# Block-sparse attention feeding a squared-ReLU layer: rounding x, whole rows' scores, one copy of fixed keys and three products with v put at other places of the issue order

## The chip, the cores and the metric

The kernel runs on one core of a Trainium2 chip. The metric is the time of one execution on the device in microseconds (us), here the median of several runs. A run of the profiler gives the trace of one execution.

## The reference

```python
scores = scale * np.matmul(q, k.transpose(0, 1, 3, 2))     # B=4, H=8, S=768, D=64
mask = np.abs(blk_i - blk_j) <= 1                           # blocks of 32: the window
mask = mask | (blk_i == 0) | (blk_j == 0) | (blk_i == n_blocks - 1) | (blk_j == n_blocks - 1)
for qb in range(n_blocks):
    for kb in sampled_blocks[qb]:                           # 3 random blocks per query block
        mask[qb * 32:(qb + 1) * 32, kb * 32:(kb + 1) * 32] = True
attn = softmax(np.where(mask, scores, -1e9))
x = (attn @ v).transpose(0, 2, 1, 3).reshape(3072, 512)
h = np.maximum(x @ w_in, 0.0)                               # 512 x 2048
return (h * h @ w_out).astype(np.float32)                   # 2048 x 512
```

The first and the last query block of each batch see every key (whole rows). Every other query block sees at most eight blocks of keys: the first, the last, three sampled ones and three of the window.

## The kernel before, in words

The 3072 tokens are 24 tiles of 128 tokens, numbered k = 0 to 23, six for each batch; three tiles make a chunk c (384 tokens, eight chunks). The attention of a tile is done in two halves of four heads, called (k, u) with u 0 or 1 (class `Half`). The whole rows of a batch are done by four pairs of heads (class `Whole`).

**The dense layer** of a chunk is the generator `moe(c)`. `turn(c)` rounds x: for each of the three tiles ScalarE (ACT) writes a rounded copy xh (line 808), and VectorE (DVE) the remainder xl (line 809). Then come 16 column blocks f. `hidden(c, f)` makes 12 matmuls on TensorE (PE, line 820) into one PSUM bank ph, then Relu on ACT (r, line 824), the square on ACT (gh, line 831), the square again on DVE (gf, line 836), and the remainder gl on GpSimd (POOL, line 838). `project(c, f)` makes 9 matmuls (line 858) with gh, gl and the split output weights, and runs two blocks behind `hidden`: the last two blocks of a chunk are projected at the start of the next `moe`. Weights are split into two parts by ACT or DVE (788, 790) and POOL (791). Chunk 0 projects unsplit (line 848).

**The order of the work is written by hand.** Each engine runs its instructions in the order in which the program issues them. `moe` yields after every piece: 4 matmuls of `hidden` or one third of `project`; a block has 6 pieces and a chunk 96. After each yield the loop counts `now` up by one and lets a `Stream` issue whatever steps of the attention are due. A `Half` or `Whole` is a generator that yields the number of pieces to its next step (`LAG`).

A `Half` of a late tile (k of 6 and above, "moved") issues: scores (line 381) and loads; after one piece the maxima (393) and the subtraction p (401), which frees the two score banks; after 4 more pieces 16 exponentials on ACT, one per piece (426), a transpose on DVE into a tile pT (432), and 11 pieces later (`v`) the products with v on PE (pv, 476), the normalization on DVE (490 to 493, 325), and the loads of v for the next tile on the DMA queue of SyncE (SP; 301, 314). In the same piece the scores of a later half are due: halves start 16 pieces apart. Before the third group of exponentials `next_keys` may copy the fixed keys (first and last block) for a coming half into its tile KG (line 288). For tiles below 6 the copy stands right behind the exponentials.

A `Whole` starts `G_AT` = 9 pieces behind a half. It issues scores (g, 567), one piece later the maxima (581 to 585), 4 pieces later two exponentials pg (592), 4 pieces later eight pieces of copies by ACT and POOL (603), 5 pieces after the last of them a transpose on DVE into a tile pTg (609), and `w` = 16 pieces later its products with v (pvg, 637) and its normalization (648 to 656). The second pair of heads also loads the other half of v (`load_vn`, 222). pT and pTg share one tag with two buffers.

Scores, ph, pv and pvg take the five banks of one PSUM pool in turn: an allocation waits until the readers of the fifth allocation before it are done.

At a chunk's end the order is: the last four matmuls of `hidden(c, 15)`, r, gh, gf, gl, a yield (so the attention steps that are due), `turn(c+1)`, three pieces of `project(c, 14)`, three of `project(c, 15)`, the output, and `hidden(c+1, 0)`, which reads xh and xl. In pieces counted through, `turn(1)` stands at piece 90, `turn(3)` at 282, `turn(5)` at 474.

Of the kernel before, what the change touches and what calls it, by code (L numbers as in the profile page):

```python
# [32 lines left out]
NF = DFF // P  # L33
# [30 lines left out]
STEP = PIECES // (2 * UC)  # L64
EARLY = 23
LAST = 4
LAG = {"s": 0, "e": 4, "v": 11, "x": 4, "t": 4, "c": 0, "v0": 13, "w0": 4, "w": 16, "n": -1}

G_AT = 9

STEP_0 = 5
STEP_1, FIRST_1 = 12, 0
LAG_1 = {**LAG, "v": 10, "x": 3, "t": 6, "v0": 5, "n": 0}
LAG_0 = {"s": 2, "x": 2, "t": 3, "c": 2, "v0": 2, "n": 2}
# [22 lines left out]
def tile_block_sparse_attention_moe(ctx: ExitStack, tc, kd, knd, qd, qgd, vd, vnd, samp, const, wcat, out):  # L97
# [9 lines left out]
    nc = tc.nc  # L107
# [7 lines left out]
    def bank(name):  # L115
        return ps.tile([P, 512], F32, tag="s", name=name)
# [167 lines left out]
    def static_keys(b, t, u, copy=nc.scalar.copy):  # L284

        src = st["kn", b, u][:, 0 : NBLK : NBLK - 1].rearrange("p i a c -> p i (a c)").unsqueeze(1)
        dst = st["kg", b, t][:, :, 0:2, 2 * u : 2 * u + 2].rearrange("p j i a c -> p j i (a c)")
        copy(dst, src.broadcast_to(list(dst.shape)))
# [40 lines left out]
    class Half:  # L329
# [10 lines left out]
        def run(self, bank, lag):  # L340

            self.scores()
            self.loads(0)
            yield lag["s"]
            self.maxima()
            if self.moved:
                yield lag["e"]
                yield from self.turn_blocks()
                yield lag["v"]
            else:  # L350
                yield lag["x"]
                self.exps()
                self.next_keys()
                yield lag["t"]
                pt = self.turn(bank)
                yield lag["c"]
                self.copies(pt)
                self.loads(1)
                yield lag["v0"]
            po = self.values(bank)  # L360
            if lag["n"] >= 0:
                yield lag["n"]
            self.norm(po)
            self.loads(2)
# [43 lines left out]
        def next_keys(self):  # L408

            b, t = order[min(self.k + self.u, len(order) - 1)]  # L410
            if b > 0 and t < 2:
                static_keys(b, t, 1 - self.u)

        def turn_blocks(self):

# [32 lines left out]
        def turn(self, bank):  # L448
            pt = [bank(f"pt{self.name}_{e}") for e in range(2)]
            n = self.rows.stop  # L450
            for e in range(2):
                for i in range(2):
                    for c in range(2):
                        a = (2 * i + c) * P
                        nc.tensor.transpose(pt[e][:, a : a + n], self.p[:n, 2 * e + i, c], ident[:n, :n])  # L455
            return pt
# [208 lines left out]
    def units(c):  # L665
# [8 lines left out]
        both = [(at + i * STEP, u) for i, u in enumerate(halves)]  # L674
        both += [(at + i * STEP + G_AT, u) for i, u in enumerate(wholes)]
        return sorted(both, key=lambda x: x[0])
# [104 lines left out]
    def need(f, part):  # L781
        while done - AHEAD - 2 <= cuts.index((f, part)):
            cut_next()

    def split(c, src, name):
        w = rot.tile([P, 2, DM], F32R, tag="w", name=name, bufs=WBUFS)
        if c == 0:
            nc.scalar.copy(w[:, 0], src)  # L788
        else:
            nc.vector.tensor_copy(w[:, 0], src)  # L790
        nc.gpsimd.tensor_tensor(w[:, 1], src, w[:, 0], op=ALU.subtract)  # L791
        return w

    def split_wo(c, f):
        if c == 0:
            need(f, 1)
            if f < PLAIN:
                return
        wo[c, f] = split(c, WO[f], f"wo{c}_{f}")
# [12 lines left out]
    def hidden(c, f):  # L812
        xh, xl = xs[c]
        wi = (wi1.pop((c, f)) if f in SINGLE else WI[f]).rearrange("p a (c m) -> p a c m", c=NCC)
        ph = bank(f"ph{c}_{f}")
        steps = []
        for cc in range(NCC):
            steps += [(wi[:, 0, cc], xh[:, cc]), (wi[:, 0, cc], xl[:, cc]), (wi[:, 1, cc], xh[:, cc])]
        for i, (w, x) in enumerate(steps):
            nc.tensor.matmul(ph[:, :TOK], w, x, start=(i == 0), stop=(i == len(steps) - 1))  # L820
            if i % 4 == 3 and i < len(steps) - 1:
                yield 0.7
        r = pool["x"].tile([P, TOK], F32, tag="r", name=f"r{c}_{f}", bufs=2)
        nc.scalar.activation(r, ph[:, :TOK], AF.Relu)  # L824
        if c == 0 and f < PLAIN:
            gt[c, f] = pool["x"].tile([P, TOK], F32, tag="gh", name=f"gp{c}_{f}", bufs=3)
            nc.scalar.activation(gt[c, f], r, AF.Square)
            yield 0.7
            return
        gh = pool["x"].tile([P, TOK], F32R, tag="gh", name=f"gh{c}_{f}", bufs=3)  # L830
        nc.scalar.activation(gh, r, AF.Square)  # L831
        gf = pool["x"].tile([P, TOK], F32, tag="gf", name=f"gf{c}_{f}", bufs=2)
        if c == 0:
            nc.scalar.activation(gf, r, AF.Square)
        else:
            nc.vector.scalar_tensor_tensor(gf, ph[:, :TOK], 0.0, r, op0=ALU.max, op1=ALU.mult)  # L836
        gl = pool["x"].tile([P, TOK], F32R, tag="gl", name=f"gl{c}_{f}", bufs=3)
        nc.gpsimd.tensor_tensor(gl, gf, gh, op=ALU.subtract)  # L838
        gt[c, f] = (gh, gl)
        yield 0.7  # L840

    def project(c, f):
        if f == 0:
            acc[c] = [ps_o.tile([P, 512], F32, tag="o", name=f"po{c}_{u}") for u in range(UC)]
        if c == 0 and f < PLAIN:
            g = gt.pop((c, f))
            for u in range(UC):
                nc.tensor.matmul(  # L848
                    acc[c][u], g[:, u * P : (u + 1) * P], WO[f], start=(f == 0), stop=(f == NF - 1)
                )  # L850
                yield 0.85
            return
        gh, gl = gt.pop((c, f))
        w = wo.pop((c, f))
        for u in range(UC):
            at = slice(u * P, (u + 1) * P)
            for i, (g, k) in enumerate(((gh, 0), (gh, 1), (gl, 0))):
                nc.tensor.matmul(  # L858
                    acc[c][u], g[:, at], w[:, k], start=(f == 0 and i == 0), stop=(f == NF - 1 and i == 2)
                )  # L860
            yield 0.68

    def emit_out(c):
        po = acc.pop(c)
        o = [rot.tile([P, DM], F32, tag="x", name=f"ot{c}_{u}", bufs=5) for u in range(UC)]
        rows = [out[(c * UC + u) * P : (c * UC + u + 1) * P] for u in range(UC)]
        if c < NCH - 1:
            for u in range(UC):
                (nc.vector.tensor_copy if u == 1 else nc.scalar.copy)(o[u], po[u])
                nc.sync.dma_start(rows[u], o[u])  # L870
            return
        nc.vector.tensor_copy(o[0], po[0])
        nc.sync.dma_start(rows[0], o[0])
        nc.scalar.copy(o[1], po[1])
        nc.scalar.dma_start(rows[1], o[1])
        for i, copy in enumerate((nc.scalar.copy, nc.vector.tensor_copy)):
            at = slice(i * DM // 2, (i + 1) * DM // 2)
            copy(o[2][:, at], po[2][:, at])
            (nc.sync if i else nc.scalar).dma_start(rows[2][:, at], o[2][:, at])

    def moe(c):


        if c < NCH:
            turn(c)
        if c > 0:
            for f in range(NF - LEAD, NF):
                if c == 1 and f == NF - 1:
                    split_wo(0, f)
                yield from project(c - 1, f)  # L890
            emit_out(c - 1)
        if c == NCH:
            return
        for f in range(NF):
            for n in (f, f + 1) if f == 0 else (f + 1,):
                if n < NF:
                    if c == 0:
                        need(n, 0)
                    if n in SINGLE:
                        wi1[c, n] = split(c, W1[n], f"wi{c}_{n}")  # L900
            if c == 0 and f > 0:
                split_wo(c, f - 1)
            if f >= LEAD:
                yield from project(c, f - LEAD)
            if c > 0:
                split_wo(c, f)
            yield from hidden(c, f)
# [59 lines left out]
    for c in range(1, NCH):  # L967
        for at, u in units(c):
            work.add(at, c, lambda u=u, lag=LAG_1 if c == 1 else LAG: u.run(bank, lag))
    now = 0  # L970
# [71 lines left out]
```

## Time and profile before

| | us |
|---|---|
| median of 3 runs | 752.5 (749.96 to 754.48) |
| the profiled execution | 753.05 |
| its span in the trace | 751.3 |
| PE busy in the span | 714.9 (95%) |
| ACT, DVE, POOL busy | 519.0, 517.4, 498.8 |

The mean granted clock of PE is 0.991. A timeline row gives the start, the time, the engine, the line, the operation, output and inputs, the count, and in brackets the idle time of the engine ahead of it with what ended it. PEld is the loading of weights, which overlaps PE. A row of waits gives who waited for whom, the total, the number of waits and the longest. A row of a stage gives its bounds and length, busy time and count of PE, PEld, DVE, ACT and POOL, the granted clock, the DMA share and GB/s. SPq is the DMA queue of SyncE.

### The profile page before, as it was taken

How to read it: one execution, taken by the hardware profiler on the slowest of the kernel's cores; microseconds unless marked ns; L12 is line 12 of the kernel's file. 1: busy time of each engine (PE TensorE's matmuls, PEld its weight loads, DVE VectorE, ACT ScalarE, POOL GpSimd, SP SyncE). 2: the span in 40 equal slices, each digit the busy share in tenths (PEclk: the TensorE clock that was granted, in tenths of full speed). 3: DMA queues.
4: the chain of work that ended last, by engine and by line, in shares of the span. 5: the costliest groups of instructions: out<-in, count | busy, mean ns of one | idle time of the engine just before them, and what ended most of it. 6: DMA issues, size and time to landing. Idle time of an engine off the chain costs nothing.

```text
span 751.3 us, 24248 instructions
## 1 busy us (share of the span) xinstructions
PE 714.9 (95%) x8904; PEld 590.0 (79%) x8904; DVE 517.4 (69%) x1060; ACT 519.0 (69%) x1145; POOL 498.8 (66%) x624
## 2 busy tenths in 40 slices
PE   4678999999899999999999999999999999999997
PEld 2556776568788888877887888886888888888986
DVE  4895977758777676667878676577869676556452
ACT  4995786898676776578886777668986785623222
POOL 6952644238667576776866576766876675777885
PEclk9998999999999999999999999999999999999999
DMA  8775789653523445534343343645244343101001
GB/s 272 223 220 144 222 237 337 172 146 91 147 53 100 131 93 170 165 84 116 98 122 105 80 131 97 214 94 142 74 121 116 82 126 73 34 1 43 1 1 43
DMA packets 85755, 92.43 MB, mean 123 GB/s; under 512 B 13539, under 2 KB 73444, under 8 KB 85636
## 3 DMA queue, kind: packets, MB, share of 16 engines
q1 hardware_dynamic: 79684, 68.03, 34.6%
q0 software_dynamic: 5664, 22.45, 8.9%
q8 instruction: 71, 1.16, 0.7%
q14 instruction: 48, 0.39, 0.2%
q10 hardware_dynamic: 288, 0.39, 0.1%
HBM read 84.53 MB, written 6.29 MB: 121 GB/s over the span
## 4 chain that ended last, share of the span: by engine, by line
PE 82%; ACT 6%; DVE 5%; DMA 3%; issue 2%; SPq 1%; POOL 1%; ACTq 0%; POOLq 0%; DVEq 0%
PE ph L820 34%; PE po L858 28%; PE s L381 7%; PE pv L476 5%; PE po L848 4%; DMA V<-in_v_dram 2%; PE pvg L637 2%; ACT pm L426 1%; PE g L567 1%; DVE m L393 1%; PE pt L455 1%; SPq L314 1%; ACT V L209 1%; DMA kn<-in_kn_dram 1%; DVE p L401 1%
## 5 line engine op out<-in xcount | busy, mean ns | idle before, releaser
L820 PE MATMUL ph<-xh,wi 128*128 128x384 f32 x832 | 238.7, 348 | 0.0
L426 ACT ACTIVATE pm<-p 32x256 f32<-32x256 f32 x528 | 219.2, 415 | 17.8 <-DVE p L401 10.7
L858 PE MATMUL po<-wo,gh 128*128 128x512 f32 x672 | 212.0, 397 | 0.0
L791 POOL TENSOR_TENSOR wi<-W,wi 128x512 fp32r<-128x512 f32 x104 | 143.3, 1378 | 68.8 <-ACT wi L788 36.2
L824 ACT ACTIVATE r<-ph 128x384 f32<-128x384 f32 x128 | 62.9, 492 | 170.5 <-PE ph L820 169.6
L791 POOL TENSOR_TENSOR wo<-WO,wo 128x512 fp32r<-128x512 f32 x112 | 145.0, 1295 | 50.8 <-DVE wo L790 49.2
L838 POOL TENSOR_TENSOR gl<-gf,gh 128x384 fp32r<-128x384 f32 x112 | 117.7, 1051 | 87.1 <-DVE gf L836 74.5
L820 PEld LDWEIGHTS ph<-xh,wi 128*128 128x128 f32 x832 | 151.2, 188 | 13.1 <-issue 5.7
L836 DVE SCALAR_TENSOR_TENSOR gf<-ph,r 128x384 f32<-128x384 f32 x112 | 62.2, 555 | 140.9 <-ACT r L824 130.0
L858 PEld LDWEIGHTS po<-wo,gh 128*128 128x128 f32 x672 | 123.7, 189 | 24.4 <-issue 5.8
L820 PE MATMUL ph<-xl,wi 128*128 128x384 f32 x416 | 141.5, 340 | 0.0
L858 PE MATMUL po<-wo,gl 128*128 128x512 f32 x336 | 133.2, 396 | 0.8 <-POOL gl L838 0.8
L820 PEld LDWEIGHTS ph<-xl,wi 128*128 128x128 f32 x416 | 78.2, 188 | 10.0 <-issue 6.5
L790 DVE CAST wo<-WO 128x512 fp32r<-128x512 f32 x112 | 84.2, 752 | 0.0
L858 PEld LDWEIGHTS po<-wo,gl 128*128 128x128 f32 x336 | 63.3, 188 | 18.1 <-POOL gl L838 4.3
L393 DVE TENSOR_REDUCE m<-s 128x2 f32<-128x512 f32 (+1 forms) x96 | 61.1, 676 | 8.8 <-PE s L381 8.7
L831 ACT ACTIVATE gh<-r 128x384 fp32r<-128x384 f32 x112 | 58.9, 526 | 9.0
L476 PEld LDWEIGHTS pv<-V,pT 128*32 128x32 f32 x2816 | 43.8, 111 | 22.7 <-issue 12.9
L476 PE MATMUL pv<-V,pT 128*32 128x65 f32 x2816 | 53.1, 223 | 7.4 <-ACT pT L465 2.9
L820 PE MATMUL ph<-xh,WI 128*128 128x384 f32 x192 | 55.1, 348 | 2.1 <-ACT xh L808 2.1
L381 PE MATMUL s<-KG,q 64*32 64x160 f32 x1408 | 50.0, 304 | 5.4 <-issue 3.6
L401 DVE TENSOR_TENSOR p<-s,m 128x512 f32<-128x512 f32 (+1 forms) x72 | 45.9, 676 | 0.0
(89 smaller groups left out, 906.9 us busy)
## 6 DMA issues: line engine op xcount, KB each, us to landing
craw<-in_w_dram POOLq DMA_DIRECT2D x32, 512.0 KB, 5.9
V<-in_v_dram SPq DMA_DIRECT2D x462, 32.5 KB, 1.9
KG<-in_k_dram SPq DMA_DIRECT2D x198, 64.0 KB, 1.9
V<-in_v_dram SPq DMA_DIRECT2D x28, 390.0 KB, 4.3
q<-in_q_dram SPq DMA_DIRECT2D x24, 256.0 KB, 2.7
out_dram<-ot SPq DMA_DIRECT2D x22, 256.0 KB, 3.7
V<-in_v_dram SPq DMA_DIRECT2D x16, 292.5 KB, 4.6
vn<-in_vn_dram SPq DMA_DIRECT2D x5, 780.0 KB, 5.6
```

The lines of the kernel that those rows point to most:

```text
L381: nc.tensor.matmul(self.sb[e][g * BLK : (g + 1) * BLK, i * NSLOT + a : i * NSLOT + z], q[r, j, pr, :], k, start=True, stop=True,)
L393: nc.vector.tensor_reduce(m[at, e], self.sb[e][at].rearrange("p (i c) -> p i c", i=2), axis=AX, op=ALU.max)
L426: nc.scalar.activation(p[a * BLK : (a + 1) * BLK, g], x[g * BLK : (g + 1) * BLK, :, a], AF.Exp, scale=SCALE)
L476: nc.tensor.matmul(po[h * BLK : (h + 1) * BLK, g * VW : (g + 1) * VW], self.pT[:, g, 2 * e + i, c], v[:, self.u, j, h * VW : (h + 1) * VW] ...
L790: nc.vector.tensor_copy(w[:, 0], src)
L791: nc.gpsimd.tensor_tensor(w[:, 1], src, w[:, 0], op=ALU.subtract)
L820: nc.tensor.matmul(ph[:, :TOK], w, x, start=(i == 0), stop=(i == len(steps) - 1))
L824: nc.scalar.activation(r, ph[:, :TOK], AF.Relu)
L831: nc.scalar.activation(gh, r, AF.Square)
L836: nc.vector.scalar_tensor_tensor(gf, ph[:, :TOK], 0.0, r, op0=ALU.max, op1=ALU.mult)
L838: nc.gpsimd.tensor_tensor(gl, gf, gh, op=ALU.subtract)
L858: nc.tensor.matmul(acc[c][u], g[:, at], w[:, k], start=(f == 0 and i == 0), stop=(f == NF - 1 and i == 2))
```

## The change

Four edits of the issue order:

1. The yield behind the last block's squares goes, and one comes in behind `turn` of the next chunk: xh and xl now follow r, gh, gf and gl directly, and the attention steps of that piece come after them. The number of pieces is the same.
2. `G_AT` goes from 9 to 6 and `w` from 16 to 19: everything of a `Whole` moves up three pieces, but its products with v stay at their piece.
3. For tiles below 6 the copy of fixed keys goes from ACT to POOL. With the condition on the batch this is one copy: the one for half (6, 0), issued by half (5, 1).
4. For the halves (7, 0), (14, 0) and (15, 0) the products with v, the normalization and the loads behind them come two pieces earlier. For (7, 0) and (14, 0) that is the piece of the products of a `Whole`, right behind them.

```diff
-LAG = {"s": 0, "e": 4, "v": 11, "x": 4, "t": 4, "c": 0, "v0": 13, "w0": 4, "w": 16, "n": -1}
+LAG = {"s": 0, "e": 4, "v": 11, "x": 4, "t": 4, "c": 0, "v0": 13, "w0": 4, "w": 19, "n": -1}
-G_AT = 9
+G_AT = 6
+APART = 2
+SPLIT = ((7, 0), (14, 0), (15, 0))
...
                 yield from self.turn_blocks()
-                yield lag["v"]
+                yield lag["v"] - APART * ((self.k, self.u) in SPLIT)
...
             if b > 0 and t < 2:
-                static_keys(b, t, 1 - self.u)
+                static_keys(b, t, 1 - self.u, nc.scalar.copy if self.moved else nc.gpsimd.tensor_copy)
...
             nc.scalar.activation(gt[c, f], r, AF.Square)
-            yield 0.7
+            if f < NF - 1:
+                yield 0.7
             return
...
         gt[c, f] = (gh, gl)
-        yield 0.7
+        if f < NF - 1:
+            yield 0.7
...
         if c < NCH:
             turn(c)
         if c > 0:
+            yield 0.7
             for f in range(NF - LEAD, NF):
```

## The prediction

> **What bounds the kernel now.** I read the page first, then PE's waits from 60 us to the end, then the timeline around each wait.
>
> ```profile
> PE 714.9 (95%) x8904; PEld 590.0 (79%) x8904; DVE 517.4 (69%) x1060; ACT 519.0 (69%) x1145; POOL 498.8 (66%) x624
> q8 instruction: 71, 1.16, 0.7%
> ```
> ```profile
> PE s L381 <- issue: 3.6, 2, 2.0
> PE s L381 <- ACT pg L592: 2.9, 3, 1.4
> PE ph L820 <- ACT xh L808: 2.1, 1, 2.1
> PE s L381 <- ACT KG L288: 1.7, 2, 1.3
> PE ph L820 <- DVE xl L809: 1.1, 3, 0.4
> PE po L858 <- POOL gl L838: 0.8, 3, 0.3
> PEld pv L476 <- issue: 10.4, 35, 0.4
> ```
>
> PE is the bound: 95% busy, and behind the first 60 us it stands still only in the first six of these waits, 12.2 us (one of them, the 2.1 us for xh, is chunk 0's own start, which the change doesn't touch). Nothing else limits: so every wait that goes shortens the span by its length, and no matmul is removed. The rest of the working goes wait by wait.
>
> **Part 4, the three products moved up.** The 3.6 us "issue" are two gaps, each ahead of the last few score matmuls of a half.
>
> ```profile
> 194.68 0.92 PE L637 MATMUL pvg<-vn,pTg 128*64 128x65 f32 x24
> 197.12 1.11 PE L476 MATMUL pv<-V,pT 128*32 128x65 f32 x64
> 198.04 0.37 SPq L222 DMA_DIRECT2D vn<-in_vn_dram  x1
> 201.30 0.46 PE L381 MATMUL s<-KG,q 64*32 64x160 f32 x3 [1.96 <-issue]
> 399.91 0.92 PE L637 MATMUL pvg<-vn,pTg 128*64 128x65 f32 x24
> 402.35 1.11 PE L476 MATMUL pv<-V,pT 128*32 128x65 f32 x64
> 406.24 0.46 PE L381 MATMUL s<-KG,q 64*32 64x160 f32 x4 [1.67 <-issue]
> ```
> ```profile
> q8 instruction: 1, 0.02, 6.0%
> q8 instruction: 1, 0.02, 7.8%
> ```
> ```profile
> 200.00:202.00 2.00, 0.70 (x4) 0.45 (x5) 0.00 (x0) 0.00 (x0) 0.00 (x0) 0.92 0.98 377
> 202.00:204.00 2.00, 2.00 (x7) 1.81 (x7) 0.11 (x1) 0.60 (x2) 0.00 (x0) 0.50 1.16 200
> 204.00:206.00 2.00, 2.00 (x8) 1.63 (x7) 2.00 (x4) 1.94 (x5) 1.36 (x3) 0.73 0.27 55
> 406.00:408.00 2.00, 1.76 (x10) 1.29 (x10) 1.30 (x3) 0.00 (x0) 0.00 (x0) 1.00 0.81 222
> ```
>
> I take both for late code. The q8 queue brought 71 packets for PE's 2 x 8904 instructions, 251 in each; the DMA view of 199 to 200 us and of 403 to 404 us holds one such packet each (the second fence). The products with v (64 matmuls and 64 loads) and the scores (the same again) are 256 instructions, and the gap comes 61 of 64 score matmuls in, so the block of code that runs out there was begun at the first product: at 197.12 and 402.35. PE used it up in 201.30 - 1.96 - 197.12 = 2.22 us (2.22 us at the second gap too), and the next block was there 4.18 and 3.89 us after the beginning. After the change the products follow pvg directly: at 194.68 + 0.92 = 195.60 instead of 197.12, 1.52 us earlier, and at 400.83 (also 1.52). Two pieces of dense matmuls (some 16 instructions) now lie between products and scores, so the block begins some 14 products' instructions later, about 0.15 us; the scores keep their time. PE has 2.22 + 1.37 = 3.59 us for a block instead of 2.22. With the same delivery 0.59 and 0.30 us of the gaps stay, with a faster one nothing: I take 0.4 (the first block is now asked for ahead of the large vn transfer at 198.04) and 0.3.
>
> Behind the first gap the clock falls: the stage rows lose 2 x (0.08 + 0.50 + 0.27) = 1.70 us of full speed; behind the second, 1.67 us long, it doesn't (1.00). With a short gap I expect no fall. [...] So (7, 0) gives 1.96 - 0.4 + 1.70 = 3.26 us (bounds 1.4 and 3.66) and (14, 0) 1.67 - 0.3 = 1.37 (bounds 1.35 and 1.67).
>
> No gap stands at (15, 0). There the products, so far back to back with the scores, get dense matmuls on either side: two more changes of shape, whose weight loads start late by 10.4 / 35 = 0.3 us each; 0 to 0.6 lost, I take 0.3. The loads of v behind the three products stay in the same order on SP's queue: at (7, 0) behind vn, which holds them at 198.04, at (14, 0) behind the key loads.
>
> **Part 2, whole rows three pieces up.**
>
> ```profile
> 333.93 0.88 PE L567 MATMUL g<-kn,QG 64*64 64x384 f32 x8
> 334.25 0.52 ACT L831 ACTIVATE gh<-r 128x384 fp32r<-128x384 f32 x1
> 335.58 1.66 ACT L808 CAST xh<-x 128x512 fp32r<-128x512 f32 x3
> 338.59 0.44 PE L820 MATMUL ph<-xl,WI 128*128 128x384 f32 x1 [0.39 <-DVE xl L809]
> 340.14 0.62 ACT L288 COPY KG<-kn 128x512 f32<-128x512 f32 x1
> 342.59 1.05 ACT L592 ACTIVATE pg<-g,mb 128x384 f32<-128x384 f32 x2
> ```
>
> The three waits for pg are PSUM banks: a half's scores come 7 pieces behind g and take the bank that the exponentials pg, issued only two pieces ahead, still read. Now they are issued five pieces ahead. Two pieces between pvg and pv took 1.52 us, so three take 2.3 us, more than the longest wait (1.4): all 2.9 us go. Next late is the copy of fixed keys: it stood one piece ahead of pg on ACT and now stands two behind it, 1.05 us later.
>
> ```profile
> 132.09 0.57 POOL L728 DMA_DIRECT2D craw<-in_w_dram  x1
> 133.26 0.62 ACT L288 COPY KG<-kn 128x512 f32<-128x512 f32 x1
> 133.94 0.57 PE L381 MATMUL s<-KG,q 64*32 64x160 f32 x10 [1.35 <-ACT KG L288]
> 136.62 1.70 POOL L791 TENSOR_TENSOR wi<-W,wi 128x512 fp32r<-128x512 f32 x1 [3.95 <-ACT wi L788]
> L288 POOL COPY KG<-kn 128x512 f32<-128x512 f32 x6 | 3.7, 609 | 5.8 <-DMA kn<-in_kn_dram 5.7
> 150.25 0.62 ACT L288 COPY KG<-kn 128x512 f32<-128x512 f32 x1
> 150.93 0.49 PE L381 MATMUL s<-KG,q 64*32 64x160 f32 x12 [0.34 <-ACT KG L288]
> 324.26 0.62 ACT L288 COPY KG<-kn 128x512 f32<-128x512 f32 x1
> 326.66 0.47 PE L381 MATMUL s<-KG,q 64*32 64x160 f32 x12
> ```
>
> At 150.93 PE waits for this copy already, so 1.05 us are lost in full there. At 326.66 the copy is done 326.66 - 324.88 = 1.78 us ahead, which covers 1.05. At the copy of 340.14 the moved xh gives most of it back; its two instances I set at 0.1 each. Part 2 gives 2.9 - 1.05 - 0.2 = 1.65 us (bounds: 2.9, and 0 if several copies are late).
>
> **Part 1, rounding x.** Between the end of gh (334.77) and xh (335.58) stand a copy and an exponential of the attention, 0.81 us, which now follow xh: the wait of 0.39 at 338.59 and its like at the other chunk boundary with whole rows, 0.7 together, go. But g, which so far lay between the two last projections there and gave gl time, now lies ahead of the last four matmuls of ph. The 0.8 us of waits for gl stand at the three boundaries that have no g; two boundaries more will wait 0.3 each. Net 0.1 us (bounds -0.6 and 0.7).
>
> **Part 3, one copy by POOL.** POOL has issued its weight load by 132.66 and next waits until 136.62; the copy is issued before that split. It ends at 132.66 + 0.61 = 133.27 instead of 133.88: 0.6 us won of 1.35. Bounds: 1.35, and a loss of over 3 us if it had to stand behind the split, which the order of issue excludes.
>
> **The sum.** 3.26 + 1.37 - 0.3 + 1.65 + 0.1 + 0.6 = 6.7 us. The profiled execution took 753.05 us (span 751.3, 1.75 around it), so 746.35. It lay 0.55 above the median of the runs, so the median goes to 745.8. All best bounds together give 3.66 + 1.67 + 2.9 + 0.7 + 1.35 = 10.3, or 742.2.
>
> **Rivals.** *The gaps aren't code, or move to another half.* If the two gaps come from something that stays, or if another block now ends in another dense stretch, 3.26 + 1.37 are missing: 2.1 us are won, 750.4. For it: the profile names no releaser. Against it: both gaps stand at the same place of the same 256 instructions, each with a packet beside it. [...]
>
> *The copies of keys eat it.* Each of twelve copies stands 1.05 us later; if eight of them cost 0.5 us, 4 us go: 749.8. Against it the margin of 1.78.
>
> *Slower: DVE waits for the buffer of pTg.* The transposes of a `Whole` move three pieces ahead of the products of the one before, and two such tiles plus a half's pT want two buffers.
>
> ```profile
> 353.27 1.01 DVE L581 TENSOR_REDUCE mg<-g 128x1 f32<-128x384 f32 x2
> 355.36 0.92 PE L637 MATMUL pvg<-vn,pTg 128*64 128x65 f32 x24
> 357.94 0.98 DVE L609 STREAM_TRANSPOSE pTg<-pgm 128x768 f32<-128x768 f32 x1 [0.30 <-POOL pgm L603]
> ```
>
> The transpose at 357.94 now comes three pieces (2.3 us) ahead of pvg and can't start before pvg ends at 356.28: a new wait of up to 0.92 + 2.3 = 3.2 us, nine times (three in each of three batches), with the normalization, gf and two weight casts queued behind it and POOL's gl and splits, hence PE, waiting for those. I count it at nothing: the maxima at 353.27, which DVE had to do in this stretch, have moved out of it, and gf's gl is needed only six pieces later. Should half of each wait show on PE, 9 x 1.6 = 14.4 us are lost and the median is 760.2; it turns slower once more than 6.7 / 9 = 0.74 us of each shows.
>
> **How the numbers follow.** A measurement of this kernel tells 0.5%, 3.8 us, from no change: 748.7 and 756.3. My forecast has 0.59, the first rival 0.20, the second 0.12, the third 0.09. The forecast is faster; of the first two rivals a quarter would still end below 748.7 (0.08); of the third 0.07 lie above 756.3. Faster 0.67, same 0.26, slower 0.07. The range runs from all best bounds, 742.2, past the first two rivals to 751.0; it leaves out the third rival and a few tails.
>
> **What would show it.** Right: no gap of 1 us or more ahead of the last score matmuls near 199 and 404 us, and a clock of 1.00 there; no wait of s for pg; the wait for KG near 133 at about 0.75 us and the one near 150 up to about 1.4; xh right behind gh. Wrong: a new "issue" gap at another half; DVE waiting for pvg ahead of line 609 together with more PE waits for gl or wi; more waits for KG.

## The result and the profile after

The kernel after takes 747.23 us (median of 11 runs, 745.98 to 749.07); the kernel before, run beside it, 752.59 (749.96 to 758.49). The ratio is 0.9926 with a 95% interval of 0.9903 to 0.995: 5.4 us faster, where 6.7 were forecast, inside the range. The profiled execution took 747.23 us with a span of 745.4, 5.9 below the span of before.

PE's waits behind the first 58 us, in the kernel after (who waited for whom, us in total, times, longest):

```profile
PE ph L823 <- ACT xh L811: 2.1, 1, 2.1
PE s L384 <- ACT KG L291: 1.9, 3, 1.2
PE po L863 <- POOL gl L842: 1.7, 5, 0.5
PE s L384 <- POOL KG L291: 0.8, 1, 0.8
PE po L863 <- ACT gh L835: 0.7, 2, 0.4
PE ph L823 <- DVE xl L812: 0.7, 1, 0.7
```

The waits add up to 7.9 us instead of 12.2. "Issue" (3.6) and pg (2.9) are gone from the list; KG, gl and gh have grown. The xl that is left is chunk 0's start, as the timeline shows:

```profile
58.37 0.44 PE L823 MATMUL ph<-xh,WI 128*128 128x384 f32 x1 [2.07 <-ACT xh L811]
59.50 0.61 PE L823 MATMUL ph<-xl,WI 128*128 128x384 f32 x1 [0.68 <-DVE xl L812]
131.89 0.65 PE L384 MATMUL s<-KG,q 64*32 64x160 f32 x10 [0.75 <-POOL KG L291]
197.73 0.82 PE L384 MATMUL s<-KG,q 64*32 64x160 f32 x16
399.04 1.08 PE L384 MATMUL s<-KG,q 64*32 64x160 f32 x16
```

Two things are to be read here. First, chunk 0's first matmul, which no edit touches, stands at 58.37; in the profile before it stood at 59.36. So 1.0 of the 5.9 us is no work of the change, and a difference of two single spans must not be taken for its effect. (In the profiles of the experiments below this matmul stands anywhere from 57.70 us, with part 1 alone, to 60.90, with part 2 alone.) Second, the last group of 16 score matmuls at the two places of the old gaps lasts 0.82 and 1.08 us where other halves need 0.58 (at 557.17, below): 0.24 and 0.50 us of the old gaps are left inside a group that counts as busy. The clock there (stages with bounds, length, busy times, then granted clock, DMA share, GB/s):

```profile
195.00:215.00 20.00, 20.00 (x331) 17.12 (x322) 15.85 (x41) 14.71 (x36) 14.38 (x18) 1.00 0.45 123
395.00:415.00 20.00, 19.92 (x351) 17.06 (x351) 12.01 (x30) 11.05 (x26) 12.80 (x11) 1.00 0.36 93
```

And the chunk boundary that the prediction took apart:

```profile
327.40 0.88 PE L570 MATMUL g<-kn,QG 64*64 64x384 f32 x8
329.79 0.53 ACT L835 ACTIVATE gh<-r 128x384 fp32r<-128x384 f32 x1
330.22 1.65 ACT L811 CAST xh<-x 128x512 fp32r<-128x512 f32 x3
333.50 0.33 PE L823 MATMUL ph<-xl,WI 128*128 128x384 f32 x1
339.68 0.49 ACT L827 ACTIVATE r<-ph 128x384 f32<-128x384 f32 x1
340.77 0.73 PE L863 MATMUL po<-wo,gh 128*128 128x512 f32 x2 [0.37 <-ACT gh L835]
341.96 0.50 PE L863 MATMUL po<-wo,gl 128*128 128x512 f32 x1 [0.46 <-POOL gl L842]
```

xh follows gh at once, and ph doesn't wait for xl any more. g stands ahead of the last matmuls of ph, and yet the projections right behind it, up to 333.5, don't wait. The new waits for gh and gl stand later, in the projection of the new chunk's first block: its r starts on ACT at 339.68, 4.1 us behind the end of its matmuls on PE (335.57; 3.3 us in the profile before), because pg, the copy of keys, two output copies and some exponentials come first there. The other boundary with whole rows shows the same waits (0.36 and 0.45).

### The profile page after: what moved, and what is told of

It is laid out like the page before. It is cut to its first block, busy times and chain, and to the rows that moved or that the text cites. A ratio compares the mean times of both kernels' runs of the same rounds, so it can differ in the third digit from the quotient of the medians.

```text
span 745.4 us, 24287 instructions
## 1 busy us (share of the span) xinstructions
PE 713.2 (96%) x8904; PEld 586.2 (79%) x8904; DVE 514.6 (69%) x1060; ACT 518.3 (70%) x1144; POOL 498.0 (67%) x625
## 3 DMA queue, kind: packets, MB, share of 16 engines
q8 instruction: 71, 1.16, 0.7%
## 4 chain that ended last, share of the span: by engine, by line
PE 85%; ACT 7%; DVE 4%; DMA 1%; issue 1%; POOL 1%; ACTq 0%; POOLq 0%; DVEq 0%
PE ph L823 35%; PE po L863 29%; PE s L384 6%; PE pv L479 6%; PE po L853 5%; PE g L570 2%; PE pvg L640 1%; ACT V L220 1%; DVE xl L812 1%; PE pt L458 1%; DMA q<-in_q_dram 1%; ACT pg L595 1%; ACT V L212 1%; POOL gl L842 1%; DMA kn<-in_kn_dram 1%
```

## The experiments

The theory: the change is worth the waits of PE that it takes away, and the two "issue" gaps are code that comes late, so that they depend on where PE's blocks of instructions end. The rivals: something else holds PE at these places; or what is won is given back by DVE's new wait, by the copies of keys or by gl.

**Part 4 alone.**

```diff
-                yield lag["v"]
+                yield lag["v"] - 2 * ((self.k, self.u) in ((7, 0), (14, 0), (15, 0)))
```

> The kernel before with part 4 alone: the products with v of the halves (7, 0), (14, 0) and (15, 0) two pieces earlier. Theory (late code blocks, two gaps in PE's issue): no gap ahead of the last score matmuls near 200 and 405 us, the clock near 202 us at 1.00; 3.3 + 1.4 - 0.3 = 4.4 us faster, span near 747. Rival (something else holds PE there): the gaps stay, under 1 us won. The waits for pg (2.9 us) and for KG (1.7 us) stay under both.

749.22 us, ratio 0.997 (0.9953 to 0.9986): 2.3 us faster, half of the 4.4 expected. Its profile has these waits as expected:

```profile
PE s L381 <- ACT pg L592: 2.9, 3, 1.4
PE s L381 <- ACT KG L288: 1.7, 2, 1.3
PE s L381 <- issue: 0.3, 1, 0.3
```

Of the two gaps 0.3 us is left, at the half where 0.30 was worked out, and pg and KG are unchanged. So the mechanism held in this execution, which took 746.39 and was the shortest of twelve (up to 752.67); the median moved less.

**Part 2 alone**: `G_AT` 9 to 6, `w` 16 to 19.

> The kernel before with part 2 alone: everything of the whole rows three pieces earlier, their products with v in place. Theory (sum of waits): the three waits of s for pg (2.9 us) go, the wait for KG near 150 us grows from 0.34 to about 1.2 and two of 0.3 to 0.4 appear at the chunk boundaries with whole rows; both issue gaps stay; about 1 us faster, which is within what can be measured. Rival (DVE's new wait for the buffer of the transpose costs PE time): slower than before, with more PE waits for gl or wi.

750.06 us, ratio 0.9974 (0.9957 to 0.9991): 2.0 us faster, where about 1 was expected.

```profile
PE s L381 <- issue: 3.3, 2, 1.7
PE s L381 <- ACT KG L288: 2.6, 2, 1.4
PE po L858 <- POOL gl L838: 1.7, 5, 0.5
```
```profile
404.06 0.47 PE L381 MATMUL s<-KG,q 64*32 64x160 f32 x6 [1.66 <-issue]
562.83 0.49 PE L381 MATMUL s<-KG,q 64*32 64x160 f32 x10 [1.67 <-issue]
```

pg is gone and gl has grown from 0.8 to 1.7, as in the kernel after. One thing was not expected: the gap near 200 us is gone without part 4, and one has come near 560, at a half where the profile before has none. The kernel isn't slower, so DVE's wait doesn't decide. The profiled execution took 752.75, next to the longest of twelve, with the late start of 60.90.

**All but part 4**: `SPLIT = ()` in the kernel after.

> The kernel after without part 4. Theory (late code blocks): the two issue gaps are back near 198 and 400 us, 3 to 4.5 us slower than the kernel after, so 750 to 751.5, 1 to 2 us faster than before. Rival (parts 1 to 3 alone remove the gaps): as fast as the kernel after, 747.

748.6 us, ratio 0.9968 (0.9949 to 0.9987): 1.4 us above the kernel after by the medians, and (0.9968 - 0.9926) x 752.6 = 3.2 us by the ratios to the runs of before made beside each. Its profile has one gap, and neither of the two old ones:

```profile
557.77 0.49 PE L384 MATMUL s<-KG,q 64*32 64x160 f32 x10 [1.67 <-issue]
```

Both theory and rival had a part wrong: the gaps of before don't come back in this execution, and yet a gap of the same kind stands elsewhere. Parts 1 to 3 alone won 2.4 us (1.0 to 3.8 by the interval). The interval of this ratio and that of the kernel after just overlap, so how much part 4 adds isn't fixed well.

**64 instructions more in the first 25 us, nothing else.**

```diff
+                    for _ in range(2 if b == 0 else 1):
                         nc.tensor.matmul(self.sg[e][...], QG[r, pr], kn[...], start=True, stop=True)
```

> The kernel before, with the score matmuls of batch 0's whole rows issued twice with the same operands into the same place (16 matmuls of two passes, so 64 PE instructions with their weight loads, all in the first 25 us). Nothing at 200 or 400 us is touched, but every later block of 251 instructions begins 64 instructions earlier in the program. Theory (late code blocks): the gaps of 1.96 and 1.67 us at these two halves go, since the block now begins in dense matmuls some 5 us ahead of the products; another half may get a gap if its block now begins at its products. Rival (data, banks or the transfers at that time hold PE): both gaps stay at the same matmuls.

753.13 us, ratio 1.0019 (1 to 1.0038). The gaps near 200 and 405 us are gone, with everything there unchanged, and a new one stands 40 us further on:

```profile
243.20 0.48 PE L381 MATMUL s<-KG,q 64*32 64x160 f32 x9 [1.69 <-issue]
```

No transfer, bank or data at 200 or 405 us was touched, only the number of instructions ahead of them, which speaks for code. That gaps vanish in one execution wouldn't settle it alone, since part 2 alone lost the first one too; the new gap does more, as it stands where the count below puts the end of a block. The profile before has 5376 PE instructions between the ends of its two gaps, from 201.30 to 406.24 us (2624 loadings of weights, 2623 matmuls, 129 separate waits), and the 21st packet of q8 behind the one that lands at 200.00 lands at 404.72: 256 instructions for each. I counted PE's instructions in the programs (a loading of weights and a matmul for each record, one for each separate wait) and took the two gaps of before as marks of where blocks of 256 end. How many of the 128 instructions of a half's scores lie ahead of such an end:

```
half             (8,0)  (15,0)  (19,0)  (20,1)
before            122    120     113     115
kernel after      120    115     108     107
64 more: (9,1) 109, (10,1) 123, (18,1) 119; none of the four above
```

The gap near 560 us stands at (20, 1), the one at 243 us at (9, 1), 9 of 64 matmuls ahead of the end of the scores (110 of 128 instructions, where 109 were counted). All the gaps of 1 us or more stand late in the scores, so that the block began at the products. That is needed and not enough: no profile shows a gap at (19, 0), where the scores of the profile before wait 1.38 us for pg anyway, nor this kernel's at (10, 1) or (18, 1). Separate waits that come or go shift the ends by a few instructions (PE has 445 in the profile before, 453 in the one after).

**Part 1 alone**: the yield behind the last squares moved behind `turn`.

> The kernel before with part 1 alone: xh and xl right behind the last squares of a chunk. Theory: the waits of ph for xl at the two chunk boundaries with whole rows (0.7 us) go, since xh starts 0.8 us earlier behind gh; g still lies between the last two projections, so no wait for gl is added there. At most 0.7 us faster, not to be told from no change by the time. Rival (attention steps that now stand behind xh and xl come late): new waits of s or pv on PE behind the boundary.

750.89 us, ratio 1.0001 (0.9972 to 1.0029), with these waits and clocks:

```profile
PE s L381 <- issue: 3.6, 2, 2.0
PE s L381 <- ACT pg L592: 3.3, 2, 1.6
PE po L860 <- POOL gl L839: 0.8, 3, 0.3
PE ph L820 <- DVE xl L809: 0.7, 1, 0.7
```
```profile
195.00:215.00 20.00, 18.05 (x338) 15.27 (x327) 12.55 (x27) 13.69 (x33) 12.75 (x17) 1.00 0.42 108
395.00:415.00 20.00, 18.31 (x219) 15.76 (x218) 12.61 (x28) 10.95 (x26) 13.06 (x12) 0.91 0.30 79
```

xl is left only at chunk 0's start, and gl has not grown: the extra waits for gl come with part 2. Of the 0.7 us won at xl, 0.4 return as longer waits for pg. The clock is the other finding: both gaps are there (3.6 us), but here the clock stays at 1.00 behind the first and falls behind the second, the reverse of the profile before.

**Part 3 alone**: the one copy by POOL.

> The kernel before with part 3 alone: one copy of fixed keys by POOL. Theory: the wait of s for KG near 133 us goes from 1.35 to about 0.75 us, now for POOL, and nothing else changes: 0.6 us, not to be told from no change by the time.

753.47 us, ratio 1.0022 (0.9993 to 1.0051). The wait for KG near 133 us is 0.75 us and for POOL, as expected. This kernel has as many PE instructions as before and its blocks end at the same places; still it shows a third gap, and no fall of the clock behind the first:

```profile
200.33 0.46 PE L381 MATMUL s<-KG,q 64*32 64x160 f32 x3 [1.60 <-issue]
403.66 0.46 PE L381 MATMUL s<-KG,q 64*32 64x160 f32 x4 [1.67 <-issue]
562.98 0.47 PE L381 MATMUL s<-KG,q 64*32 64x160 f32 x6 [1.57 <-issue]
```
```profile
195.00:215.00 20.00, 18.40 (x342) 15.61 (x343) 12.81 (x32) 14.82 (x36) 13.61 (x18) 1.00 0.40 108
```

So the position decides where a gap can stand, and the execution whether it does and whether the clock falls.

The DMA records of the traces show the code itself. Behind 58 us the profiles of the kernel before and of the experiments have 21 gaps of PE called "issue" (0.32 to 2.22 us), and every one ends 1.30 to 1.58 us after a 16 KB packet of the instruction queue q8 has landed (in the profile before the packets land at 200.00 and 404.72, and PE goes on at 201.30 and 406.24). There are only 71 packets, so such stretches of 0.28 us make up 20 of some 750 us: this is no chance. The packets also show why one execution has a gap and another not. At (20, 1) the packet starts 1.11 us ahead of the first product in the profile before, and no gap follows; with part 3 alone it starts 1.05 us behind it, and PE stands still for 1.57. Without a split, all 13 gaps of 1 us or more go with a packet that started 1.03 to 1.92 us behind the first product; in the halves that a kernel splits, with packets up to 2.04 us behind it, at most 0.62 us are left. What makes the packet start sooner or later stays open.

The clock can be taken further too. In each trace its changes lie a whole number of steps of 3.413 us apart: in the profile before those at 37.82, 41.24, 58.30, 65.13, 201.66 and 205.07 us lie 6, 7, 12, 14, 54 and 55 such steps behind the one at 17.34. Two such steps with a gap of the profile before, each with the step behind it:

```profile
198.25:201.66 3.41, 1.46 (x64) 0.91 (x64) 1.52 (x6) 0.00 (x0) 1.27 (x1) 1.00 0.84 278
201.66:205.07 3.41, 3.41 (x10) 3.00 (x10) 1.18 (x3) 1.63 (x4) 0.47 (x1) 0.50 0.86 166
403.05:406.46 3.41, 1.74 (x95) 1.24 (x83) 1.69 (x6) 2.32 (x6) 2.55 (x3) 1.00 0.36 87
406.46:409.87 3.41, 3.41 (x20) 2.98 (x17) 2.82 (x5) 0.00 (x0) 0.18 (x1) 1.00 0.53 144
```

PE was idle for 1.95 us of the first step, and the clock stood at 0.50 for the whole next one, a loss of 1.7 us; it was idle for 1.67 us of the third, and nothing fell. From 80 us to the end of PE's work the thirteen profiles have three falls, and they follow the three steps with the most idle time: 1.95 here, 1.69 with part 1 alone, 2.22 in the kernel with keys ahead of pg. The gap of 1.96 us with part 1 alone was cut by the end of a step into 1.51 and 0.45, and cost no clock. So in these three about half a step or more was idle inside one step. This is read off afterwards, from three falls, and is no bound: 1.67 us had no fall where 1.69 had one, and ahead of 80 us a step with 1.72 idle had none either (in the kernel with the transposes put back).

**The transposes of whole rows put back**: `w0` 4 to 7 and `w` 19 to 16 in the kernel after.

> The kernel after with the transposes of the whole rows put back to their piece (5 more pieces become 8 behind the copies, products with v unchanged). Theory (DVE's wait for the buffer is hidden): DVE's waits of line 609's transpose for pvg, 9.2 us in six, go, and the time stays within 1 us of the kernel after. Rival (that wait reaches PE through gl): PE's waits for gl fall from 1.7 to under 1 us and the kernel is 1 to 3 us faster than the kernel after.

749.44 us, ratio 0.9978 (0.9954 to 1.0002). DVE's waits in the kernel after,

```profile
DVE pTg L612 <- PE pvg L640: 9.2, 6, 1.6
DVE pTg L612 <- POOL gl L842: 5.6, 3, 1.9
```

are both gone here, and PE's wait for gl is the same to the tenth:

```profile
PE s L384 <- issue: 2.0, 2, 1.4
PE po L863 <- POOL gl L842: 1.7, 5, 0.5
```

So the new wait is real, as the slower rival had it, and doesn't reach PE through gl. The time is not within the 1 us expected: 2.2 us above the kernel after by the medians and (0.9978 - 0.9926) x 752.6 = 3.9 us by the ratios, whose intervals don't overlap. In the two profiled executions the gaps explain it: from chunk 0's first matmul to the end they take 689.2 and 687.0 us, and 2.0 us of gaps are back. Whether they explain the medians stays open.

**Keys ahead of pg**: `if g == 2:` becomes `if g == 1:` ahead of `next_keys` in the kernel after.

> The kernel after with each copy of fixed keys issued four pieces earlier, ahead of the exponentials pg on ACT. Theory: the three waits of s for ACT's KG copy (1.2, 0.4 and 0.3 us) go, 1.9 us in all, and no wait for pg comes back, since pg is still issued four pieces ahead: about 1.5 to 2 us faster than the kernel after, 745 to 746. Rival (another ACT step takes the place): waits for pg or gh grow by as much and the time stays.

746.33 us, ratio 0.9917 (0.9886 to 0.9949). All three waits for ACT's copies are gone, and those for gh too. The median is 0.9 us below that of the kernel after, less than the 1.5 to 2 expected, and the intervals overlap. The profiled execution was the longest of nine (749.84; the shortest took 742.44): the gap at (20, 1) takes 2.2 us there, and the clock falls behind it.

```profile
PE s L384 <- issue: 2.2, 1, 2.2
PE po L863 <- POOL gl L842: 1.7, 5, 0.5
```
```profile
556.33:559.75 3.42, 1.20 (x17) 0.81 (x14) 1.68 (x4) 0.00 (x0) 1.91 (x2) 1.00 0.61 156
559.75:563.16 3.41, 3.41 (x12) 3.32 (x11) 1.95 (x4) 0.35 (x1) 0.00 (x0) 0.50 0.27 52
```

**A fourth half, (19, 1), moved up**: `SPLIT = ((7, 0), (14, 0), (15, 0), (19, 1))`.

> The kernel after with a fourth half's products moved up two pieces, (19, 1), ahead of the scores of (20, 1). Counting PE's instructions in the program, the block of 256 that holds the products of (19, 1) and the scores of (20, 1) ends 107 of 128 instructions into these scores in the kernel after, and the gap stood there (near 560 us) in the kernels with part 2 alone, without part 4, and with part 3 alone. Theory (late code blocks): no gap of 0.5 us or more at any half in any profile of this kernel, and 0 to 1.7 us faster than the kernel after, since there the gap comes in some executions only. Rival (the gap moves on to the next dense half whatever is split): another gap of 1 us or more behind 560 us.

747.9 us, ratio 0.9944 (0.9921 to 0.9967): not faster than the kernel after, as far as the intervals tell. No wait is called "issue" in its profile, but three groups of score matmuls hold some 0.5 us each. The profile of the kernel after happens to have no gap at (20, 1) (first fence); the fourth split leaves half a microsecond there in its own (second):

```profile
557.17 0.58 PE L384 MATMUL s<-KG,q 64*32 64x160 f32 x16
```
```profile
558.01 1.07 PE L384 MATMUL s<-KG,q 64*32 64x160 f32 x16
```

**Keys ahead of pg, and (19, 1) in place of (15, 0).**

> The kernel after with the copies of fixed keys ahead of pg on ACT, and (19, 1) in place of (15, 0) among the three products moved up. Theory: PE's waits for ACT's KG copy (1.9 us) and the gap near 560 us go, nothing comes back: 1.5 to 3 us faster than the kernel after, 743.5 to 745.5. Rival (waits for pg, gh or gl grow in their place): as fast as the kernel after.

745.7 us, ratio 0.9909 (0.9879 to 0.9939), the shortest of all; the kernel with the fourth split, on the same chip, took 747.9. Some of PE's waits there:

```profile
PE po L863 <- POOL gl L842: 1.7, 5, 0.5
PE ph L823 <- issue: 0.7, 1, 0.7
PE s L384 <- issue: 0.4, 1, 0.4
```

No wait for ACT's copies, and 0.4 us of the gap at (20, 1): as expected. Not expected was a gap of 0.72 us in ph, at 426.90. The median is 1.5 us below that of the kernel after, 0.2 outside the range expected. Its interval overlaps that of the kernel after, so that it beats it is likely, not shown.

**The same with `G_AT` 7 and `w` 18.**

> As the one before, with the whole rows two pieces up instead of three (7 and 18 in place of 6 and 19), so that at a chunk boundary g stands behind the rounding of x again. Theory: the waits of po for gh (0.7 us) go and those for gl fall from 1.7 to about 0.8 us, without a wait for pg coming back, since pg stands four pieces ahead of the scores: 1 to 1.6 us faster than the one before, 742.5 to 744.5. Rival (four pieces are too few): one or two waits of s for pg of 0.5 us or more, and no gain.

747.13 us, ratio 0.9925 (0.9898 to 0.9952): no gain. No wait for pg came back, but neither did gl fall:

```profile
PE po L863 <- POOL gl L842: 2.0, 7, 0.4
PE po L863 <- issue: 0.6, 1, 0.6
PE ph L823 <- issue: 0.6, 1, 0.6
```

The waits for gl now stand in part at other blocks (7 of them), which the expectation did not see. At the two boundaries with whole rows they did fall, from 0.46 us each to 0.16 and to nothing, and three of 0.35 came elsewhere.

## Why the prediction was right, point by point

**The bound.** PE was the bound (busy for 713.2 of 745.4 us in the profile after), and waits taken away shortened the time. The kernel's parts add up roughly: 0.30% for part 4 and 0.32% for parts 1 to 3 against 0.74% together, each with an interval of some 0.2% either way. Taken from chunk 0's first matmul to the end, the two profiled executions differ by 4.9 us, and nearly all of it is the gaps (2.9 of 3.6 us gone) and the clock (1.7): the other waits together changed by less than 1 us.

**Parts 1 to 3** were put at 0.1 + 1.65 + 0.6 = 2.35 us, and all but part 4 won 2.4. This agreement is in part luck. pg's 2.9 us went in full, and the copy by POOL waits 0.75, as worked out (0.6 won). But the copy behind pg near 150 us costs 1.16 instead of 0.34, and two others 0.36 and 0.34 where 0.1 each was set: part 2 comes to 2.9 - 0.8 - 0.7 = 1.4 instead of 1.65. Part 1 with g's place comes to 0.7 - 0.9 - 0.7 = -0.9 instead of 0.1: xl's 0.7 went, gl took 0.9 (from 0.8 to 1.7 where 1.4 was forecast), and gh took 0.7, which was not foreseen. By the waits the three parts are worth 1.4 - 0.9 + 0.6 = 1.1 us. The rest of the 2.4 has another source; the gaps are the likely one, since the profile without part 4 has lost both old ones and got one new, but this isn't shown.

The step behind this is "g, which so far lay between the two last projections there and gave gl time, now lies ahead of the last four matmuls of ph". The two boundaries did get their wait for gl, but not at those projections: r, gh, gf and gl of the next chunk's first block are late, because ACT has pg and the copy of keys ahead of r there. Once PE no longer waits for pg, it comes sooner to the next thing that ACT delivers. With the copies of keys issued earlier the waits for gh went. How much of gl's lateness belongs to pg and how much to the other work of ACT wasn't taken apart.

**Part 4** is the largest term that was mis-sized: "(7, 0) gives 1.96 - 0.4 + 1.70 = 3.26 us". What is left of the two gaps, 0.24 and 0.50 us, is near the 0.4 and 0.3 set, and the profile after has the clock at 1.00 there. But the term was read from one execution as if every one had it. The clock falls behind the first gap in the profile before, behind the second with part 1 alone, behind none with part 3 alone. Part 4 alone moved the median by 2.3 us where 4.3 were put, and in the kernel after it is worth 1.4 us by the medians or 3.2 us by the ratios, both below the 4.3. In the profile of parts 1 to 3 neither old gap stands: the packets there started 0.74 and 1.47 us ahead of the first product. Whether the shift of the blocks or the execution did that isn't shown.

**The rivals.** "The gaps aren't code" fell with the shift by 64 instructions; "or move to another half" came true in part: (20, 1), which the change doesn't split, has the gap in five of the experiments' kernels. The waits for ACT's copies of keys that part 2 moved grew by 1.5 us in all, not 4. DVE's wait for the buffer came at the nine transposes, 9.2 us in six and 5.6 behind POOL in three, and cost PE nothing visible: putting the transposes back left the wait for gl at 1.7. The reasons that the prediction gave for this were not tested one by one.

**Open** is what decides in an execution when a packet of code starts; what of the gaps and of the clock is in the medians, of which the profiles are single draws; and what, if anything, moving (15, 0) costs: no gap was seen at the scores of (16, 0) with or without it.

## What to carry to other kernels

A wait that the profile calls "issue" on a busy engine, without a releaser, is worth a look at the instruction transfers: here each such gap ended 1.30 to 1.58 us behind one. A shift by a few dozen harmless instructions far ahead is a second test of code against data; since a gap can also be absent by chance, look for where the new one stands, and not only for the old one to go. When such a gap is mended by moving one dense stretch, count where the next block ends, since an edit ahead of it can move it. When a wait goes, ask what the engine will wait for next: here PE gave back at gh and gl part of what it won at pg. A loss that hangs on one execution's state, such as a clock that fell, belongs in the range and not in full in the sum: look at a second profile first.

## What the hardware did that was not expected

In the profile before PE used up 255 and 252 instructions in 2.22 us each, from the first product to the gap. In seven of eleven experiments PE stood still for 1.4 to 2.2 us late in the scores of a half, each time up to 1.30 to 1.58 us behind the landing of a packet of q8. The same program positions gave a gap of 1.57 us in one execution and none in another, (20, 1) with part 3 alone and before, as the packet of code started 1.05 us behind the first product or 1.11 us ahead of it.

The clock fell behind gaps of 1.96, 1.69 and 2.22 us in three profiles, each time to 0.50 for 3.41 us, and stayed at 1.00 behind others of 1.37 to 1.96 us. The falls went with where the idle time met the steps of 3.413 us: 1.95 us of it lay inside one step at the first gap of the profile before, and the gap of 1.96 without a fall, with part 1 alone, was cut into 1.51 and 0.45.
